# Attention into routed experts: first keys prepared in two column blocks, some of the opening work moved to GpSimd

## The chip, the cores and the metric

One core of a Trainium2 chip. The metric is the device time of one execution in microseconds (us). The engines are named as the profile names them: PE (TensorE matmuls) and PEld (its weight loads), DVE (VectorE), ACT (ScalarE), POOL (GpSimd), SP (SyncE, here a DMA queue). A q behind a name (SPq, ACTq, POOLq) is the engine's queue, from which it issues DMAs.

## What is computed

Attention over q, k, v of shape (8, 12, 448, 64), with queries and keys normalised over their 64 features, then a layer of eight experts that keeps at most 80 tokens per expert:

```python
def rmsnorm(x, g):
    return x / np.sqrt(np.mean(x * x, axis=-1, keepdims=True) + 1e-06) * g
scores = np.matmul(rmsnorm(q, g_q), rmsnorm(k, g_k).transpose(0, 1, 3, 2)) / np.sqrt(64)
attn = softmax(scores)                       # batch 8, heads 12, 448 x 448
x = matmul(attn, v)                          # to 3584 rows of 768
logits = x @ w_gate                          # 8 experts, the best one per row
# each expert keeps the 80 rows of the highest gate weight
out[rows] = gate * (np.maximum(x[rows] @ w1[e], 0) @ w2[e])
```

The product g_q * g_k / 8 is one vector over the 64 features. It can stand on either side of the score product, so the kernel applies it once, to one of the two.

## The kernel before

The attention goes in 24 groups (NG) of four heads. One tile of a group is 128 partitions by 14 blocks (NB) of 64 features: 64 row positions of two heads lie on the partitions, and the 14 blocks are two halves (head pairs `hh`) of seven columns x (NX). For each group:

- `load_qk` (line 259) loads q and k. The four buffers of the tag `qk` go round, so the load for group g+2 waits until group g's tile has been read. All these loads but two halves of group 0 are in SP's queue, in program order.
- `square` (278, ACT) and `squares` (285, DVE) make the sums of squares; `root` (293, ACT) and `inverse` (307, DVE) make 1/rms for group 0, `rstd` (298) does it for later groups by Ln and Exp on ACT and three small DVE operations; `normalise` (312, DVE) multiplies.
- `transp` (340) turns the normalised tile with 14 PE transposes into PSUM and copies it to `T0` (queries) or `T1` (keys) in SBUF. For group 0 the keys' copy, on DVE (line 355), applies the vector `gqk`.
- `score` (361) takes one column block x of keys: four matmuls into a PSUM tile `ps` (two buffers of the tag `sc`), then the exponential on ACT into `at`. `av` (375) multiplies `at` by v; `presum` (397, DVE) adds up the seven `at` tiles.

The order of the program is written out by hand. Slots s run from -10 to 89; slot s issues scores 2s and 2s+1, then the functions listed under `mid`, then the value products 2s-2 and 2s-1, then those under `end`. Lists `begins`, `mid`, `end`, `ahead` and `after` are filled by `at_slot`. Each engine works through its own instructions in program order.

Slot -10 (lines 721 to 728) prepares group 0 and, on ACT, squares the first tile of group 1 (`square(1, 0)`). Queries and keys of group 0 are squared, summed and normalised in halves `lo` and `hi`. `load_g` (81) has two small loads of g_q and g_k in ACT's queue; `gains` (88) multiplies them on POOL and turns the row into a PSUM column `gp` with a small matmul, `gained` (98) copies it to `gqk`. `exptable` (715) has ACT load its exponential table. PE begins with 12 matmuls on zeros (line 806, tile `wps`), and `stir` (101) issues more of them, three and two, between the transposes. Group 1 is squared, normalised and turned in slots -1 to 2, group 2 from slot 0 on.

While group 0 is being prepared, POOL sets constants (lines 126 to 175 and the identity for the transposes); `constants` (158) has DVE convert some of them.

Of the kernel before, what the change touches and what calls it, by code (L numbers as in the profile page):

```python
# [10 lines left out]
F32 = mybir.dt.float32  # L11
BF16 = mybir.dt.bfloat16
AF = mybir.ActivationFunctionType
# [8 lines left out]
def kernel(  # L22
# [13 lines left out]
    nc = tc.nc  # L36

    B, H, S, D = q.shape
# [9 lines left out]
    NX = S // 64  # L48
# [7 lines left out]
    NB = 2 * NX  # L56
# [7 lines left out]
    NW0 = 3  # L64
    wb_dram = nc.dram_tensor("wb_scratch", (E - NW0, 2, DM * F), BF16, kind="Internal").ap()

    cpool = ctx.enter_context(tc.tile_pool(name="const", bufs=1))

    warm = cpool.tile([1, 2], F32, name="warm")
# [9 lines left out]
    gk = []  # L79

    def load_g():
        gk.append(tpool.tile([128, 512], F32, tag="R", name="gk"))
        for t, src in enumerate((g_q, g_k)):
            nc.scalar.dma_start(
                out=gk[0][:1, t * 128:t * 128 + 128].rearrange("p (t d) -> p t d", t=2),
                in_=src[None, None, :].to_broadcast([1, 2, D]))

    def gains():

        t = gk[0]  # L90
        grow = t[:1, 256:384]
        nc.gpsimd.tensor_mul(grow, t[:1, 0:128], t[:1, 128:256])
        nc.gpsimd.tensor_scalar_mul(grow, grow, 1.0 / math.sqrt(D))
        gp = scps.tile([128, 2, 512], F32, tag="sc", name="gp")
        nc.tensor.matmul(gp[:, 0, 0:1], grow, one[:, :], start=True, stop=True)
        gk.extend((gp, wps))
# [30 lines left out]
    ZW = 192  # L127
    zeros = cpool.tile([128, ZW], F32, name="zeros")
    nc.vector.memset(zeros[:, :], 0.0)

    tpool = ctx.enter_context(tc.tile_pool(name="topk", bufs=1))

# [98 lines left out]
    tpps = ctx.enter_context(tc.tile_pool(name="tp_ps", bufs=1, space=PSUM))  # L231
# [3 lines left out]
    scps = ps_stack.enter_context(tc.tile_pool(name="sc_ps", bufs=2, space=PSUM))  # L235
# [9 lines left out]
    with av_stack:  # L245
# [3 lines left out]
        st = [dict() for _ in range(NG)]  # L249
# [28 lines left out]
        def square(g, a, parts=ALLB):  # L278
            if "sq%d" % a not in st[g]:
                st[g]["sq%d" % a] = qkpool.tile([128, NB, D], F32, tag="sq", name="sq", bufs=2)  # L280
            for lo, hi in parts:
                nc.scalar.activation(st[g]["sq%d" % a][:, lo:hi], st[g]["qk"][a][:, lo:hi],  # L282
                                     AF.Square)

        def squares(g, a, parts=ALLB):
            if "ms" not in st[g]:
                for n in ("ms", "rs", "nw"):
                    st[g][n] = prep.tile([128, 2, NB], F32, tag=n, name=n)
            for lo, hi in parts:
                nc.vector.reduce_sum(out=st[g]["ms"][:, a, lo:hi],  # L290
                                     in_=st[g]["sq%d" % a][:, lo:hi], axis=AX.X)

        def root(g, a, parts):
            for lo, hi in parts:
                nc.scalar.activation(st[g]["rs"][:, a, lo:hi], st[g]["ms"][:, a, lo:hi], AF.Sqrt,
                                     scale=1.0 / D, bias=eps[:, :])

        def rstd(g):
# [7 lines left out]

        def inverse(g, a, parts):
            for lo, hi in parts:
                rs = st[g]["rs"][:, a, lo:hi]
                nc.vector.reciprocal(rs, rs)  # L310

        def normalise(g, a, parts=ALLB):
            if "qn%d" % a not in st[g]:
                st[g]["qn%d" % a] = qkpool.tile([128, NB, D], F32, tag=f"qn{a}", name="qn", bufs=2)
            qn, qk, rs = st[g]["qn%d" % a], st[g]["qk"][a], st[g]["rs"][:, a]
            for lo, hi in parts:
                h0, h1 = lo // NX, hi // NX
                nc.vector.tensor_mul(  # L318
                    qn[:].rearrange("p (x hh) d -> p hh x d", hh=2)[:, h0:h1],
                    qk[:, lo:hi].rearrange("p (hh x) d -> p hh x d", x=NX),  # L320
                    rs[:, lo:hi].rearrange("p (hh x) -> p hh x", x=NX)
                    .unsqueeze(3).to_broadcast([128, h1 - h0, NX, D]))

        def turned(o, w, p):
            one = ident if w.dtype == F32 else identb
            nc.tensor.transpose(o, w, one[p, p], tile_position=(p.start, 0))  # L326
# [13 lines left out]
        def transp(g, a):  # L340

            if not a or g == 1:
                tp = tpps.tile([128, 2, 512], F32, tag="tp", name="tp")
            else:
                tp = scps.tile([128, 2, 512], F32, tag="sc", name="tp")
            qn = st[g]["qn%d" % a]
            T = qktpool.tile([128, 2, S], F32, tag=f"qkT{a}", name="qkT")
            st[g]["T%d" % a] = T
            for x in range(NX):
                for u in range(2):  # L350
                    p = slice(64 * u, 64 * u + 64)
                    turned(tp[:, u, x * 64:(x + 1) * 64],
                           qn[p, 2 * x:2 * x + 2, :].rearrange("p h d -> p (h d)"), p)
            if g == 0 and a:
                nc.vector.tensor_scalar_mul(T[:], tp[:, :, :S], gqk[:, :])
            elif a == (g == 0):
                nc.scalar.activation(T[:], tp[:, :, :S], AF.Copy, scale=gqk[:, :])  # L357
            else:
                nc.scalar.copy(T[:], tp[:, :, :S])  # L359

        def score(r):
            g, x = divmod(r, RD)
            T0, T1 = st[g]["T0"], st[g]["T1"]
# [343 lines left out]
        def at_slot(where, s, f, *a):  # L707
            where.setdefault(s, []).append((f, a))
# [11 lines left out]
        lo, hi = HALF  # L720
        for f, *a in ((square, 0, lo), (square, 0, hi), (squares, 0, lo), (root, 0, lo),
                      (square, 1, lo), (squares, 0, hi), (root, 0, hi), (square, 1, hi),
                      (lambda: square(1, 0), ), (inverse, 0, lo), (normalise, 0, lo), (inverse, 0, hi),
                      (normalise, 0, hi), (squares, 1, lo), (root, 1, lo), (squares, 1, hi),
                      (root, 1, hi), (transp, 0), (gains, ), (stir, 3, 2), (inverse, 1, lo),
                      (normalise, 1, lo), (inverse, 1, hi), (normalise, 1, hi), (gained, ),
                      (exptable, ), (transp, 1), (stir, 2, 1)):
            at_slot(mid, -10, f, *([0] if a and f is not stir else []), *a)
        for g in range(NG):
            b0 = g * RD // 2  # L730
            at_slot(begins, b0 - 11 if g > 1 else -10, load_qk, g)
            at_slot(begins, b0 - 4, load_v, g)
            if g:
                for a in range(2):
                    if a or g > 1:
                        at_slot(mid, b0 - 7 + a if g > 1 else -1, square, g, a)
                    at_slot(end, b0 - 7 + a if g > 1 else -1, squares, g, a)
                at_slot(mid, b0 - 5 if g > 1 else 0, rstd, g)
                for a in range(2):
                    s = b0 - 5 + a if g > 1 else 0  # L740
# [325 lines left out]
```

## Time and profile before

| | us |
|---|---|
| median of 3 runs | 418.39 |
| lowest and highest | 416.96, 419.76 |
| the profiled execution | 416.07 |
| span of its instructions | 414.4 |
| PE busy in the span | 399.3 |
| DVE busy | 355.9 |
| ACT busy | 315.4 |
| POOL busy | 82.0 |

The span runs from the first to the last instruction; 1.67 us of the profiled execution lie outside it. "Busy" counts instructions in work on an engine; a matmul's duration holds its passage through the array, so a string of matmuls overlaps. Rows give times from the start of the span.

### The profile page before, as it was taken

The page shows a single profiled execution, that of the slowest core. Times are in us where ns is not written, and L with a number is a line of the kernel's source. Part 1 is how long each engine was busy: PE and PEld are TensorE (multiplying, and loading weights), DVE is VectorE, ACT ScalarE, POOL GpSimd, SP SyncE. Part 2 cuts the span into 40 slices and gives each one's busy share as a digit, 9 for nine tenths or more (in the row PEclk, how much of TensorE's full clock was granted, in tenths as well). Part 3 has the DMA queues.
Part 4 walks back from the last instruction along what each step waited for, and adds up shares of the span by engine and source line. Part 5 has one row for each costly group of instructions (what it writes and reads, how often), then busy time and mean ns, then how long its engine had stood idle before and what let it go on. Part 6 is the DMA issues. An engine that isn't in the chain of part 4 may idle for free.

```text
span 414.4 us, 12611 instructions
## 1 busy us (share of the span) xinstructions
PE 399.3 (96%) x5299; PEld 196.8 (47%) x5299; DVE 355.9 (86%) x656; ACT 315.4 (76%) x482; POOL 82.0 (20%) x140
## 2 busy tenths in 40 slices
PE   8999999999999999999999999999999999889993
PEld 8434444444444445444443444444344444448882
DVE  7799887998999999989999999979999969735560
ACT  6898979997989699979899699978997784402111
POOL 3000002501040013121241025101502030134321
PEclk9999999999999999999999999999999999999997
DMA  7469998999989899989999999999899294989981
GB/s 261 143 163 227 260 322 170 277 218 294 245 235 276 226 256 270 295 187 251 245 314 225 235 265 267 255 228 303 206 228 292 54 338 165 258 256 341 346 297 47
DMA packets 75983, 100.91 MB, mean 244 GB/s; under 512 B 8344, under 2 KB 65176, under 8 KB 75928
## 3 DMA queue, kind: packets, MB, share of 16 engines
q1 hardware_dynamic: 59856, 70.53, 53.1%
q0 software_dynamic: 15776, 29.13, 38.8%
q8 instruction: 41, 0.67, 0.6%
q10 hardware_dynamic: 296, 0.46, 0.4%
q14 instruction: 14, 0.11, 0.1%
HBM read 101.11 MB, written 39.89 MB: 340 GB/s over the span
## 4 chain that ended last, share of the span: by engine, by line
PE 85%; DVE 4%; ACT 4%; DMA 3%; issue 2%; POOLq 0%; DVEq 0%
PE ps L369 30%; PE po L386 28%; PE zl L421 5%; PE py L1014 4%; PE tp L326 4%; PE ph L995 3%; PE xp L326 3%; DMA qk<-in_k_dram 2%; PE wps L806 2%; ACT at L372 1%; DMA xg<-xr_scratch,idxG 1%; PE mp L599 1%; ACT zsb L431 1%; ACT zo L433 1%; DVE sm L404 1%
## 5 line engine op out<-in xcount | busy, mean ns | idle before, releaser
L372 ACT ACTIVATE at<-ps 128x896 f32<-128x896 f32 x168 | 146.4, 930 | 4.8 <-PE ps L369 3.7
L369 PE MATMUL ps<-qkT 64*64 64x448 f32 x1344 | 147.2, 548 | 3.0 <-ACT row L553 1.3
L386 PE MATMUL po<-at,vt 64*64 64x448 f32 x1344 | 142.4, 537 | 0.0
L404 DVE TENSOR_TENSOR sm<-sm,at 128x896 f32<-128x896 f32 x120 | 130.5, 1087 | 3.1
L386 PEld LDWEIGHTS po<-at,vt 64*64 64x64 f32 x1344 | 50.0, 133 | 74.5 <-issue 64.5
L369 PEld LDWEIGHTS ps<-qkT 64*64 64x64 f32 x1344 | 43.4, 132 | 67.6 <-issue 25.8
L290 DVE TENSOR_REDUCE ms<-sq 128x14 f32<-128x896 f32 (+1 forms) x50 | 51.9, 1042 | 5.2 <-ACT sq L282 5.2
L318 DVE TENSOR_TENSOR qn<-qk,rs 128x896 f32<-128x896 f32 (+1 forms) x50 | 52.4, 1049 | 1.4
L282 ACT ACTIVATE sq<-qk 128x896 f32<-128x896 f32 (+1 forms) x50 | 46.3, 930 | 1.7 <-DMA qk<-in_q_dram 1.7
L999 ACT ACTIVATE h_sb<-ph 128x320 bf16<-128x320 f32 x16 | 7.0, 438 | 37.5 <-PE ph L995 37.5
L213 POOL COPY mark<-mark 1x1 bf16<-1x1 bf16 x20 | 7.5, 375 | 138.2 <-DVE mark L212 138.2
L666 ACT COPY xb<-xp 128x1024 f32<-128x1024 f32 x24 | 24.3, 1012 | 9.0 <-PE xp L326 8.6
L326 PEld LDWEIGHTS tp<-ident,qn 64*128 64x128 f32 x672 | 23.4, 139 | 11.4 <-ACT at L372 4.9
L326 PE MATMUL tp<-ident,qn 64*128 64x64 f32 x672 | 26.9, 226 | 0.1
L393 ACT COPY us<-po 128x896 f32<-128x896 f32 (+1 forms) x24 | 21.4, 894 | 6.9 <-PE po L386 6.9
L402 DVE TENSOR_TENSOR sm<-at 128x896 f32<-128x896 f32 x24 | 26.0, 1084 | 0.1
L357 ACT ACTIVATE qkT<-tp,gqk 128x896 f32<-128x896 f32 x23 | 23.6, 1025 | 0.0
L359 ACT COPY qkT<-tp 128x896 f32<-128x896 f32 x24 | 22.0, 917 | 1.5 <-PE tp L326 1.4
L1014 PE MATMUL py<-w_sb,h_sb 128*80 128x384 bf16 (+1 forms) x136 | 22.2, 317 | 0.0
L1018 DVE TENSOR_SCALAR yo<-py,gwT 80x384 f32<-80x384 f32 (+1 forms) x16 | 9.5, 601 | 13.9 <-PE py L1014 13.6
L421 PE MATMUL zl<-us,wgs 64*32 64x448 f32 x192 | 20.4, 540 | 0.0
L421 PE MATMUL zl<-sm,zsel 64*32 64x448 f32 x192 | 20.3, 540 | 0.0
(176 smaller groups left out, 425.1 us busy)
## 6 DMA issues: line engine op xcount, KB each, us to landing
wb_scratch<-in_moe_w_dram POOLq DMA_DIRECT2D x20, 768.0 KB, 10.3
w_sb<-wb_scratch SPq DMA_DIRECT2D x9, 1536.0 KB, 9.8
vt<-in_v_dram SPq DMA_DIRECT2D x24, 448.0 KB, 5.5
out_dram<-zeros SPq DMA_DIRECT2D x28, 384.0 KB, 9.0
qk<-in_q_dram SPq DMA_DIRECT2D x23, 448.0 KB, 5.7
qk<-in_k_dram SPq DMA_DIRECT2D x23, 448.0 KB, 5.9
w_sb<-in_moe_w_dram POOLq DMA_DIRECT2D x6, 1536.0 KB, 14.2
xr_scratch<-xb SPq DMA_DIRECT2D x48, 192.0 KB, 7.5
```

Source lines behind the costliest of these rows:

```text
L282: nc.scalar.activation(st[g]["sq%d" % a][:, lo:hi], st[g]["qk"][a][:, lo:hi], AF.Square)
L290: nc.vector.reduce_sum(out=st[g]["ms"][:, a, lo:hi], in_=st[g]["sq%d" % a][:, lo:hi], axis=AX.X)
L318: nc.vector.tensor_mul(qn[:].rearrange("p (x hh) d -> p hh x d", hh=2)[:, h0:h1], qk[:, lo:hi].rearrange("p (hh x) d -> p hh x d", x=NX), ...
L326: nc.tensor.transpose(o, w, one[p, p], tile_position=(p.start, 0))
L369: nc.tensor.matmul(ps[u * 64:u * 64 + 64, hh, :S], T1[d, u, x * 64:(x + 1) * 64], T0[d, u, :], start=True, stop=True)
L372: nc.scalar.activation(at[:], ps[:, :, :S], AF.Exp)
L386: nc.tensor.matmul(po[u][hh * D:(hh + 1) * D, u, :S], vt[p, hh * NX + x, :], at[p, hh, :], start=(x == 0), stop=(x == RD - 1))
L402: nc.vector.tensor_add(s["sm"][:], s["at0"][:], s["at1"][:])
L404: nc.vector.tensor_add(s["sm"][:], s["sm"][:], s["at%d" % x][:])
L421: nc.tensor.matmul(t[32 * c:32 * c + 32, r, :S], w, x, start=(i == 0), stop=(i == NQ - 1))
L666: nc.scalar.copy(xb[:].rearrange("p j (u hh d) -> p hh (j u) d", u=2, hh=2), xp[:].rearrange("p hh (k d) -> p hh k d", d=D))
L1014: nc.tensor.matmul(py[:, :c1 - c0], h_sb[:, fc, :], chunk(e, 1, fc)[:, c0:c1], start=(fc == 0), stop=(fc == FC - 1))
```

## The change

The two loads of g_q and g_k are issued by POOL, ahead of all its constants. The second half of group 0's queries is normalised on POOL; the product of the gains follows it on POOL, and its small matmul becomes a function of its own (`gproduct`). Group 1's squares are both made on POOL, in slot -10. Group 0's keys are summed in halves as before, get one reciprocal, and are then normalised, turned and copied in two blocks of columns: three columns (`keys_normal(0)`, `keys_turned(0)`) ahead of the first score, four with `keys_normal(1)` in slot -10 and `keys_turned(1)` in slot 0, behind scores 0 and 1. Score x of group 0 takes the block that holds its column. One zero matmul stands where three stood, and one where two stood. `rstd` and the normalising of group 1 go from slot 0 to slot 1; its queries' transposes go ahead of slot 2's value products; group 2's squares, `rstd` and normalising go one slot later.

```diff
+    tpool = ctx.enter_context(tc.tile_pool(name="topk", bufs=1))
+    def load_g():
+        gk.append(tpool.tile([128, 512], F32, tag="R", name="gk"))
+        for t, src in enumerate((g_q, g_k)):
+            nc.gpsimd.dma_start(
...
+    load_g()
     cpool = ctx.enter_context(tc.tile_pool(name="const", bufs=1))
...
-            nc.scalar.dma_start(
...
         nc.gpsimd.tensor_scalar_mul(grow, grow, 1.0 / math.sqrt(D))
+
+    def gproduct():
+        grow = gk[0][:1, 256:384]
         gp = scps.tile([128, 2, 512], F32, tag="sc", name="gp")
         nc.tensor.matmul(gp[:, 0, 0:1], grow, one[:, :], start=True, stop=True)
...
-    def stir(n, t):
-        for i in range(n):
-            nc.tensor.matmul(gk[t][:, 1, :ZW], zeros[:, :128], zeros[:, :], start=True, stop=True)
+    def stir(t):
+        nc.tensor.matmul(t[:, 1, :ZW], zeros[:, :128], zeros[:, :], start=True, stop=True)
...
-                nc.scalar.activation(st[g]["sq%d" % a][:, lo:hi], st[g]["qk"][a][:, lo:hi],
-                                     AF.Square)
+                o, x = st[g]["sq%d" % a][:, lo:hi], st[g]["qk"][a][:, lo:hi]
+                if g == 1:
+                    nc.gpsimd.tensor_mul(o, x, x)
+                else:
+                    nc.scalar.activation(o, x, AF.Square)
...
-                nc.vector.tensor_mul(
+                e = nc.gpsimd if g == 0 and h0 else nc.vector
+                e.tensor_mul(
...
+        KP = ((0, 3), (3, NX))
+        def keys_normal(n):
+            x0, x1 = KP[n]
...
+            nc.vector.tensor_mul(
+                qn[:].rearrange("p (x hh) d -> p hh x d", hh=2)[:, :, x0:x1],
+                st[0]["qk"][1][:].rearrange("p (hh x) d -> p hh x d", x=NX)[:, :, x0:x1],
+                st[0]["nw"][:, 1].rearrange("p (hh x) -> p hh x", x=NX)[:, :, x0:x1]
+                .unsqueeze(3).to_broadcast([128, 2, x1 - x0, D]))
+        def keys_turned(n):
...
+            for x in range(x0, x1):
+                for u in range(2):
+                    p = slice(64 * u, 64 * u + 64)
+                    turned(tp[:, u, x * 64:(x + 1) * 64],
+                           st[0]["qn1%d" % n][p, 2 * x:2 * x + 2, :].rearrange("p h d -> p (h d)"),
+                           p)
+            c = slice(64 * x0, 64 * x1)
+            nc.vector.tensor_scalar_mul(T[:, :, c], tp[:, :, c], gqk[:, :])
...
-                      (lambda: square(1, 0), ), (inverse, 0, lo), (normalise, 0, lo), (inverse, 0, hi),
-                      (normalise, 0, hi), (squares, 1, lo), (root, 1, lo), (squares, 1, hi),
-                      (root, 1, hi), (transp, 0), (gains, ), (stir, 3, 2), (inverse, 1, lo),
-                      (normalise, 1, lo), (inverse, 1, hi), (normalise, 1, hi), (gained, ),
-                      (exptable, ), (transp, 1), (stir, 2, 1)):
+                      (inverse, 0, lo), (normalise, 0, lo), (inverse, 0, hi),
+                      (normalise, 0, hi), (gains, ), (squares, 1, lo), (root, 1, lo), (squares, 1, hi),
+                      (root, 1, hi), (transp, 0), (lambda: stir(wps), ), (gproduct, ), (inverse, 1, ALLB),
+                      (keys_normal, 0), (gained, ), (keys_turned, 0), (exptable, ), (lambda: stir(gk[1]), ),
+                      (keys_normal, 1), (lambda: square(1, 0), ), (lambda: square(1, 1), ),
+                      (lambda: squares(1, 0), )):
...
+        at_slot(mid, 0, keys_turned, 1)
+        at_slot(mid, 0, squares, 1, 1)
...
-                at_slot(mid, b0 - 5 if g > 1 else 0, rstd, g)
+                late = g == 2
+                for a in range(2 if g > 1 else 0):
+                    at_slot(mid, b0 - 7 + a + late, square, g, a)
+                    at_slot(end, b0 - 7 + a + late, squares, g, a)
+                at_slot(mid, b0 - 5 + late if g > 1 else 1, rstd, g)
...
-                    at_slot(end, b0 - 2 + (a if g == 1 else 0), transp, g, a)
+                    if g == 1:
+                        at_slot(end if a else mid, b0 - 1, transp, g, a)
+                    else:
+                        at_slot(end, b0 - 2, transp, g, a)
...
-        at_slot(begins, -10, load_g)
```

## Rows read from the trace of the kernel before

**Rows 1.** The page: busy time by engine, granted clock by slice, the chain that ended last.

```profile
PE 399.3 (96%) x5299; PEld 196.8 (47%) x5299; DVE 355.9 (86%) x656; ACT 315.4 (76%) x482; POOL 82.0 (20%) x140
...
PEclk9999999999999999999999999999999999999997
...
PE 85%; DVE 4%; ACT 4%; DMA 3%; issue 2%; POOLq 0%; DVEq 0%
```

**Rows 2.** Timeline of PE: start, length, engine, line, out<-in, count [idle before <-releaser].

```profile
1.59 6.84 PE L806 MATMUL wps<-zeros 128*128 128x192 f32 x24 [1.59 <-DVE zeros L129]
8.36 0.65 PE L326 MATMUL tp<-ident,qn 64*128 64x64 f32 x14
9.00 0.38 PE L95 MATMUL gp<-one,gk 1*128 1x1 f32 x2
...
10.61 0.65 PE L326 MATMUL tp<-ident,qn 64*128 64x64 f32 x14
...
12.60 1.73 PE L369 MATMUL ps<-qkT 64*64 64x448 f32 x16 [0.49 <-DVE qkT L355]
14.61 1.79 PE L369 MATMUL ps<-qkT 64*64 64x448 f32 x16 [0.28 <-ACT at L372]
...
21.58 0.65 PE L326 MATMUL tp<-ident,qn 64*128 64x64 f32 x14
...
31.66 1.08 PE L326 MATMUL tp<-ident,qn 64*128 64x64 f32 x28
```

**Rows 3.** Timeline of DVE, the opening and group 2's keys.

```profile
2.62 0.89 DVE L163 CAST numF<-numI 128x8 f32<-128x8 int32 x1
5.06 1.15 DVE L290 TENSOR_REDUCE ms<-sq 128x7 f32<-128x448 f32 x2 [1.56 <-ACT sq L282]
...
6.35 0.62 DVE L318 TENSOR_TENSOR qn<-qk,rs 128x448 f32<-128x448 f32 x1
...
7.66 1.14 DVE L290 TENSOR_REDUCE ms<-sq 128x7 f32<-128x448 f32 x2
...
9.72 0.63 DVE L318 TENSOR_TENSOR qn<-qk,rs 128x448 f32<-128x448 f32 x1
...
11.30 1.15 DVE L355 TENSOR_SCALAR qkT<-tp,gqk 128x896 f32<-128x896 f32 x1 [0.89 <-PE tp L326]
...
27.45 1.08 DVE L318 TENSOR_TENSOR qn<-qk,rs 128x896 f32<-128x896 f32 x1
```

**Rows 4.** Timeline of ACT around its table load.

```profile
9.06 0.91 ACT L359 COPY qkT<-tp 128x896 f32<-128x896 f32 x1
9.98 1.28 ACT L716 ACT_TABLE_LOAD   x1
...
13.64 1.73 ACT L372 ACTIVATE at<-ps 128x896 f32<-128x896 f32 x2 [1.32 <-PE ps L369]
```

**Rows 5.** Timeline of POOL in the opening.

```profile
3.19 0.29 POOL L170 TENSOR_SCALAR_AFFINE_SELECT tri<-tri 128x128 bf16<-128x128 bf16 x1
7.84 0.45 POOL L92 TENSOR_TENSOR gk<-gk 1x128 f32<-1x128 f32 x1 [4.37 <-DMA gk<-in_g_k_dram]
8.38 0.56 POOL L93 TENSOR_SCALAR gk<-gk 1x128 f32<-1x128 f32 x1
```

**Rows 6.** Groups of instructions on POOL: count | busy us, mean ns | idle before.

```profile
L216 POOL DMA_DIRECT2D wb_scratch<-in_moe_w_dram x20 | 15.3, 763 | 0.7
...
L522 POOL TENSOR_TENSOR info<-eq,pt 128x160 bf16<-128x160 f32 x8 | 3.9, 482 | 0.6
```

**Rows 7.** Timeline of DVE and POOL at 334 to 338 us.

```profile
334.21 2.19 DVE L404 TENSOR_TENSOR sm<-sm,at 128x896 f32<-128x896 f32 x2
...
335.41 1.05 POOL L529 TENSOR_TENSOR left<-gw,pt 128x4 f32<-128x4 f32 x1
...
336.80 0.21 POOL L531 TENSOR_TENSOR pt<-left,pt 128x4 bf16<-128x4 f32 x1
```

**Rows 8.** Stretches: length, busy (count) of PE, PEld, DVE, ACT, POOL, granted clock, DMA share, GB/s.

```profile
12.00:13.00 1.00, 0.51 (x6) 0.24 (x9) 1.00 (x2) 0.32 (x1) 0.00 (x0) 1.00 1.03 384
...
60.00:100.00 40.00, 39.89 (x542) 17.20 (x540) 36.11 (x61) 35.95 (x52) 7.53 (x10) 1.00 0.99 244
```

More of the change, by code (lines that the diff above doesn't have):

```diff
@@ L77 @@
     nc.vector.memset(one[:, :], 1.0)
[L79 to L83, printed above, removed]
-            nc.scalar.dma_start(
-                out=gk[0][:1, t * 128:t * 128 + 128].rearrange("p (t d) -> p t d", t=2),
-                in_=src[None, None, :].to_broadcast([1, 2, D]))
     def gains():
@@ L294, in root @@
             for lo, hi in parts:
-                nc.scalar.activation(st[g]["rs"][:, a, lo:hi], st[g]["ms"][:, a, lo:hi], AF.Sqrt,
+                nc.scalar.activation(st[g][("rs", "nw")[a]][:, a, lo:hi],
+                                     st[g]["ms"][:, a, lo:hi], AF.Sqrt,
                                      scale=1.0 / D, bias=eps[:, :])
@@ L308, in inverse @@
             for lo, hi in parts:
-                rs = st[g]["rs"][:, a, lo:hi]
+                rs = st[g][("rs", "nw")[a]][:, a, lo:hi]
                 nc.vector.reciprocal(rs, rs)
@@ L322, in normalise @@
                     .unsqueeze(3).to_broadcast([128, h1 - h0, NX, D]))
+        KP = ((0, 3), (3, NX))
+        def keys_normal(n):
+            x0, x1 = KP[n]
+            qn = qkpool.tile([128, NB, D], F32, tag="qn1", name="qn", bufs=2)
+            st[0]["qn1%d" % n] = qn
+            nc.vector.tensor_mul(
[4 more added lines that the diff above has]
+        def keys_turned(n):
+            x0, x1 = KP[n]
+            if n:
+                tp = tpps.tile([128, 2, 512], F32, tag="tp", name="tp")
+            else:
+                tp = scps.tile([128, 2, 512], F32, tag="sc", name="tp")
+            T = qktpool.tile([128, 2, S], F32, tag="qkT1", name="qkT")
+            st[0]["T1%d" % n] = T
+            for x in range(x0, x1):
[6 more added lines that the diff above has]
+            nc.vector.tensor_scalar_mul(T[:, :, c], tp[:, :, c], gqk[:, :])
         def turned(o, w, p):
@@ L353, in transp @@
                            qn[p, 2 * x:2 * x + 2, :].rearrange("p h d -> p (h d)"), p)
-            if g == 0 and a:
-                nc.vector.tensor_scalar_mul(T[:], tp[:, :, :S], gqk[:, :])
-            elif a == (g == 0):
+            if g and not a:
                 nc.scalar.activation(T[:], tp[:, :, :S], AF.Copy, scale=gqk[:, :])
@@ L362, in score @@
             g, x = divmod(r, RD)
-            T0, T1 = st[g]["T0"], st[g]["T1"]
+            T0 = st[g]["T0"]
+            T1 = st[g]["T1" if g else "T1%d" % (x >= KP[1][0])]
             ps = scps.tile([128, 2, 512], F32, tag="sc", name="ps")
@@ L722 @@
                       (square, 1, lo), (squares, 0, hi), (root, 0, hi), (square, 1, hi),
-                      (lambda: square(1, 0), ), (inverse, 0, lo), (normalise, 0, lo), (inverse, 0, hi),
-                      (normalise, 0, hi), (squares, 1, lo), (root, 1, lo), (squares, 1, hi),
-                      (root, 1, hi), (transp, 0), (gains, ), (stir, 3, 2), (inverse, 1, lo),
-                      (normalise, 1, lo), (inverse, 1, hi), (normalise, 1, hi), (gained, ),
-                      (exptable, ), (transp, 1), (stir, 2, 1)):
-            at_slot(mid, -10, f, *([0] if a and f is not stir else []), *a)
+                      (inverse, 0, lo), (normalise, 0, lo), (inverse, 0, hi),
[4 more added lines that the diff above has]
+                      (lambda: squares(1, 0), )):
+            own = f in (keys_normal, keys_turned)
+            at_slot(mid, -10, f, *([0] if a and not own else []), *a)
+        at_slot(mid, 0, keys_turned, 1)
+        at_slot(mid, 0, squares, 1, 1)
         for g in range(NG):
@@ L733 @@
             if g:
-                for a in range(2):
-                    if a or g > 1:
-                        at_slot(mid, b0 - 7 + a if g > 1 else -1, square, g, a)
-                    at_slot(end, b0 - 7 + a if g > 1 else -1, squares, g, a)
-                at_slot(mid, b0 - 5 if g > 1 else 0, rstd, g)
-                for a in range(2):
-                    s = b0 - 5 + a if g > 1 else 0
+                late = g == 2
[3 more added lines that the diff above has]
+                at_slot(mid, b0 - 5 + late if g > 1 else 1, rstd, g)
+                for a in range(2):
+                    s = b0 - 5 + a + late if g > 1 else 1
                     at_slot(after if not a and g % NQ == 0 and g > NQ else mid, s, normalise, g, a)
```

7 lines of the change are left out of this document (5 added, 2 removed).

## The prediction

> **What bounds the kernel now.** I read the page first, then the timelines of the opening engine by engine, then the stretches. On the page PE is busy for 96% of the span and carries 85% of the chain that ended last [rows 1]. From 60 to 100 us it is busy for 39.89 of 40 us while the DMA engines are busy throughout, so there it waits for no transfer [rows 8]. An edit that touches the first slots alone can therefore move the end only by bringing PE's unbroken run forward, and what it brings forward there should arrive at the end almost unchanged. The place to read is where that run starts.
>
> Before 12.60 PE does warm-up, transposes and zero matmuls; the first scores start at 12.60, 0.49 after PE's last work, released by the keys' copy on DVE [rows 2]. That copy (11.30, 1.15 long) follows the transposes of 10.61, and these follow DVE's multiply of 9.72 to 10.35 [rows 2, 3]. DVE is then the bound of the opening: from 5.06 to 10.35 it works through sums, reciprocals and four multiplies almost without a gap, starting when ACT hands over the first squares [rows 3]. The second pair of scores starts at 14.61, released by the exponentials, which began at 13.64 [rows 2, 4]. So the stage to re-time is DVE's from 5 to 12 us, then whatever DVE and POOL owe to PE up to 31.66, where group 2's transposes stand [rows 2].
>
> **The opening on DVE and POOL.** The second query multiply (0.62, some 0.55 in a pipelined string) leaves DVE, so the two key sums (1.14) start at 7.1 instead of 7.66 and end at 8.25 [rows 3]. From the first sum's end (half of 1.15 after 5.06, that is 5.65) to its multiply at 6.35 lie 0.7 us for root, reciprocal and hand-overs [rows 3]; so the first keys' multiply could start at 8.95. It has 384 elements where the half had 448: 0.56 by proportion. The one reciprocal of 14 in place of two of 7 changes nothing beyond that.
>
> POOL's price is not in the trace for this size. A two-input operation of four elements took 0.21 when nothing stood against it and one of 160 took 0.48 [rows 6, 7]; the line through both is 0.2 plus 1.75 ns an element, so 1.0 for 448 and 1.75 for 896. Below, I bound it by the single-row operation of 128 elements at 0.45 as a fixed price (0.45 and 0.45) [rows 5]; above, by proportion to the 160 (1.35 and 2.7) [rows 6]. I take 1.0 and 1.85, nearest to the line. The Trainium skill (GPSIMD Engine Reference, Performance versus the Vector engine) holds such work to be VectorE's and gives 4497 ns for 2048 elements; by it, as an estimate, 896 cost 1.97, 0.1 more than I take.
>
> The query half then runs on POOL from 7.15 to 8.15. PE cannot turn the queries before 8.36 anyway, because its warm-up lasts until then [rows 2], so this multiply is hidden; without that cover it would delay only the queries, whose copy ends at 9.97 and is not needed before the first score [rows 4]. The gains follow on POOL, 1.10 for the pair (7.84 to 8.94 before) [rows 5]: 8.15 to 9.25. The gain loads, which held them until 7.84, are no longer on the path.
>
> **The shared resource.** In the stretch at 334 us a four-element operation of POOL issued at 335.41 lasted 1.05, until DVE's pair of two-input additions had ended at 336.40; right after, its like took 0.21 [rows 7]. The other way round, a DVE cast of eight elements took 0.89 and ended at 3.51, when POOL's last constant ended at 3.48 [rows 3, 5]. I read this as: one of the two waits while the other has an operation in hand. The Trainium skill (Advanced Engine Details and Errata, GPSIMD Details) says that Pool shares a read and a write interface with DVE and conflicts with its operations of two SBUF inputs. The rows agree for POOL waiting; that a multiply of DVE waits for a long operation of POOL is in no row, and it is the choice on which my size hangs.
>
> I take it that it does. Then the first keys' multiply waits for the gains: 9.25 to 9.85. Six transposes by proportion to 14 in 0.65, with the last one's passage, 0.4: to 10.3 [rows 2]. The copy of 384 from PSUM, scaled from 1.15 for 896, 0.6: to 10.9 [rows 3]. First score at 10.95 against 12.60 [rows 2]: 1.65 earlier. The exponential table is loaded by 11.26 [rows 4] and the first score needs about 1.04 to its exponential (12.60 to 13.64), so 12.0: the load stays hidden, with some 0.7 left for the small exponential behind it.
>
> **Between the first scores and group 1.** Behind scores 0 and 1 (to 12.7) PE has eight transposes of the second key block, 0.4, then score 2 at 13.1. POOL squares group 1's queries from 9.85 to 11.7; `keys_normal(1)` (512 elements, 0.7) waits for it: to 12.4. Then `squares(1, 0)` stands ahead of the second block's copy in DVE's queue: 1.05, to 13.45, and the copy (0.7) ends at 14.15. Score 3 waits for it, about 0.15 behind PE. Value products start at 15.0; before, PE reached them at 14.61 + 1.6 = 16.2 [rows 2]. So 1.2 are left: added waits that were absent before, on POOL and in DVE's queue, take 0.45 of the 1.65.
>
> POOL's second square runs 12.4 to 14.25, its sum to 15.3, one addition to 16.35, the small operations of `rstd` to 17.2, the multiply of group 1's queries to 18.25. PE finishes scores 4 and 5 at 18.0, so their transposes wait 0.25. They now stand ahead of the value products; the keys' transposes come at 20.4 against 21.58 [rows 2]: 1.15 earlier.
>
> For group 2, DVE has from 19.3 on ten operations of about 1.05 and 0.7 of small ones until the keys of group 2 are ready: 30.5. Before, they were ready at 28.53 [rows 3] and turned at 31.66 [rows 2]; with PE 1.15 earlier they are wanted at 30.5. The cover of 3.1 us is used up by the move of one slot, and any further lateness of DVE shows there. On SP's queue the load of the third group's queries waits for POOL's half (8.15), its keys' load for `keys_normal(1)`: 12.4, two later than the last multiply of 10.35 [rows 3]; both are first needed after 16 us. The loads behind them follow; nothing reads them before slot 3.
>
> **Edits at nothing.** Issuing the gain loads on POOL: 0.76 for one of 768 KB [rows 6], bounded below by the 0.21 of the smallest POOL operation and above by twice 0.76; two push POOL's constants, and with them DVE's casts, which ended at 3.51, by 0.4 to 3.0, of which 1.55 are free before 5.06 [rows 3]. I take 1.5: no cost. The squares and the DMA issues that ACT loses were not on the path. The three zero matmuls fewer leave PE idle in pieces below a microsecond; the clock is granted in full also in the stretch where PE was busy for 0.51 of 1 us [rows 8]. Later stages do not change.
>
> **Sum.** 1.65 - 0.45 - 0.1 = 1.1 us off the profiled execution's 416.07, so 415.0 (span 413.3). The median of the runs shown is 418.39, 2.3 above that execution, and the forecast is for a median: 417.3. About 1% (4.2 us) is what a measurement of this kernel can tell from no change; this is a quarter of it.
>
> **Rivals.** *DVE does not wait for POOL.* Then the first keys' multiply ends at 9.5, the gains' column lands at 9.65, scores start at 10.7, group 1's transposes wait little, and group 2 is ready 0.6 sooner: 1.7 off, 416.7. For it: DVE's two-input additions kept their usual length beside POOL at 334 us [rows 7]; against it: the cast of 0.89 [rows 3]. Chance 0.22.
>
> *POOL's squares become the bound (the other side).* Two squares in series stand before group 1's `rstd`. Each 0.1 us more apiece costs about 0.2 at group 1's transposes; the gain of 1.1 is gone at 2.4 us each, and at 2.7, the proportional bound [rows 6], the kernel is 0.6 slower: 419.0. For it: POOL's four-element operation of 1.05 beside DVE [rows 7]; against it: the line through the unhindered ones. Chance 0.18.
>
> *POOL's opening DMAs are dear.* At 1.1 each (0.76 is the mean with 768 KB [rows 6]) the casts end at 5.7, the sums start 0.65 late, and 0.45 is left: 417.9. Chance 0.12. *The clock falls* when PE idles between small pieces: 32 score matmuls of 1.73 and 1.79 [rows 2] at half speed, of which the exponentials' pace hides some 1.5: 2 lost, 0.9 slower, 419.3. The full grant at half occupancy speaks against it [rows 8]. Chance 0.05.
>
> *The gain is given back later*, because DVE (86% busy [rows 1]) falls behind at group 2 or at a buffer: no change, 418.4. Chance 0.08. My own case keeps 0.35.
>
> **How the numbers follow.** All cases lie between 416.7 and 419.3; the three runs of before spread over 2.8, so a median is uncertain by about 1 either way. Range 415.0 to 419.4; my own case alone 416.2 to 418.4. Below 414.2 needs more than all the opening's idle time gives (0.07); above 422.6 needs POOL at several times its bound or a long spell at low clock (0.04); within 1%: 0.89.
>
> **What would show it.** First score near 10.95, DVE's keys' multiply lengthened or delayed to POOL's end, a POOL square near 1.85, group 1's key transposes near 20.4, group 2's near 30.5, and PE unbroken after. Wrong if POOL's 896 exceed 2.4, if DVE's first sum starts past 5.3, if the granted clock drops below full before 20 us, or if the lead at 31 us is lost by 100 us.

## The result and the profile after

The changed kernel took 423.32 us (median of 6 runs, 421.95 to 424.82) against 417.42 for the kernel before (median of 6; the 418.39 above is that of its first 3): ratio 1.0132, 95% interval 1.0098 to 1.0166. It is slower by 1.3%, where the forecast was 1.1 us faster. The profiled execution took 421.95, its span is 420.2 against 414.4.

PE's timeline shows where. The columns are those of [rows 2].

```profile
8.29 0.65 PE L363 MATMUL tp<-ident,qn 64*128 64x64 f32 x14 [0.37 <-POOL qn L326]
...
13.15 0.58 PE L363 MATMUL tp<-ident,qn 64*128 64x64 f32 x6 [3.38 <-DVE gqk L104]
...
14.78 3.27 PE L405 MATMUL ps<-qkT 64*64 64x448 f32 x16
...
18.59 2.24 PE L405 MATMUL ps<-qkT 64*64 64x448 f32 x16
...
26.43 0.65 PE L363 MATMUL tp<-ident,qn 64*128 64x64 f32 x14
...
36.51 1.08 PE L363 MATMUL tp<-ident,qn 64*128 64x64 f32 x28
```

PE stood still for 3.38 us ahead of the first keys' transposes. The first scores start at 14.78 (12.60 before), and the pair takes 3.27 instead of 1.73. Group 1's keys are turned at 26.43 instead of 21.58, group 2's at 36.51 instead of 31.66: 4.85 late. From there little more is lost for 290 us (0.24, then 0.05 regained): the first gate matmuls of the eight batches come 5.09 late (61.76 against 56.67), the last 5.04 (353.34 against 348.30). The remaining 0.8 of the span's 5.8 lie behind that, 0.5 of them in the first gather of rows (4.01 against 3.49), which takes between 3.49 and 4.33 over the profiles of all these kernels.

The bracket names the copy of the gains' column, and that copy only stood in DVE's queue behind something else. DVE's timeline, to be read against [rows 3]:

```profile
5.18 1.15 DVE L296 TENSOR_REDUCE ms<-sq 128x7 f32<-128x448 f32 x2
...
7.12 1.09 DVE L296 TENSOR_REDUCE ms<-sq 128x7 f32<-128x448 f32 x2
...
8.86 4.15 DVE L338 TENSOR_TENSOR qn<-qk,nw 128x384 f32<-128x384 f32 x1
12.93 0.14 DVE L104 COPY gqk<-gp 128x1 f32<-128x1 f32 x1
13.77 0.62 DVE L359 TENSOR_SCALAR qkT<-tp,gqk 128x384 f32<-128x384 f32 x1 [0.70 <-PE tp L363]
14.31 0.68 DVE L338 TENSOR_TENSOR qn<-qk,nw 128x512 f32<-128x512 f32 x1
```

The first keys' multiply was ready at 8.86, as forecast (8.95), and lasted 4.15. Its sister of 512 elements, larger, lasted 0.68. The difference stands in POOL's timeline:

```profile
7.29 0.94 POOL L326 TENSOR_TENSOR qn<-qk,rs 128x448 f32<-128x448 f32 x1 [1.97 <-DVE rs L317]
...
8.74 0.56 POOL L95 TENSOR_SCALAR gk<-gk 1x128 f32<-1x128 f32 x1
9.28 3.31 POOL L287 TENSOR_TENSOR sq<-qk 128x896 f32<-128x896 f32 x2
```

POOL's two squares run from 9.28 to 12.59, and the multiply ends at 13.01, 0.42 later. By the profile the multiply had started first, 0.42 before the squares, and that did not help it. The clock then shows in the stretches (columns of [rows 8]):

```profile
12.00:13.00 1.00, 0.00 (x0) 0.00 (x0) 1.00 (x2) 0.00 (x0) 0.59 (x1) 0.92 0.00 0
13.00:14.00 1.00, 0.85 (x7) 0.76 (x8) 0.30 (x3) 0.00 (x0) 0.00 (x0) 0.50 0.00 0
...
18.00:19.00 1.00, 1.00 (x15) 0.78 (x16) 0.29 (x1) 0.90 (x1) 0.00 (x0) 0.50 0.81 301
...
20.00:21.00 1.00, 1.00 (x16) 0.34 (x12) 1.00 (x2) 0.85 (x2) 0.00 (x0) 1.00 0.08 16
```

The granted clock fell while PE still stood (0.92 over the stretch from 12 to 13) and is 0.50, that is 1.2 GHz of 2.4, until past 19 us. So the theory after the result has two links: DVE's multiply of two SBUF inputs waits for POOL's run of operations as a whole, not for the one in hand; and PE's standstill then costs it half its clock for the first scores.

### The profile page after: what moved, and what is told of

The parts are those of the page before. It is cut to its first block, busy times and chain, and to the rows that moved or that the text cites. A ratio compares the mean times of both kernels' runs of the same rounds, so it can differ in the third digit from the quotient of the medians.

```text
span 420.2 us, 12599 instructions
## 1 busy us (share of the span) xinstructions
PE 401.0 (95%) x5293; PEld 196.1 (47%) x5293; DVE 358.7 (85%) x655; ACT 314.0 (75%) x480; POOL 87.2 (21%) x145
## 4 chain that ended last, share of the span: by engine, by line
PE 86%; ACT 5%; DVE 4%; issue 2%; DMA 1%; POOL 1%; POOLq 0%
PE ps L405 32%; PE po L422 29%; PE zl L457 5%; PE py L1056 4%; PE tp L363 4%; PE xp L363 3%; PE ph L1037 3%; ACT at L408 2%; DVE qn L338 1%; DMA xg<-xr_scratch,idxG 1%; PE mp L635 1%; ACT zsb L467 1%; ACT zo L469 1%; ACT xb L702 1%; PE mp L363 1%
## 5 line engine op out<-in xcount | busy, mean ns | idle before, releaser
L405 PE MATMUL ps<-qkT 64*64 64x448 f32 x1344 | 149.3, 554 | 2.3 <-ACT row L589 1.3
L326 DVE TENSOR_TENSOR qn<-qk,rs 128x896 f32<-128x896 f32 (+1 forms) x47 | 50.5, 1076 | 1.3
L289 ACT ACTIVATE sq<-qk 128x896 f32<-128x896 f32 (+1 forms) x48 | 44.5, 930 | 1.9 <-DMA qk<-in_q_dram 1.9
```

Source lines behind the costliest of these rows:

```text
L289: nc.scalar.activation(o, x, AF.Square)
L326: e.tensor_mul(qn[:].rearrange("p (x hh) d -> p hh x d", hh=2)[:, h0:h1], qk[:, lo:hi].rearrange("p (hh x) d -> p hh x d", x=NX), rs[:, lo ...
L405: nc.tensor.matmul(ps[u * 64:u * 64 + 64, hh, :S], T1[d, u, x * 64:(x + 1) * 64], T0[d, u, :], start=True, stop=True)
```

## The experiments

**The squares back on ACT.** All else stays as changed; the first square stands where it stood before the change, the second in slot 0.

```diff
-                if g == 1:
-                    nc.gpsimd.tensor_mul(o, x, x)
-                else:
-                    nc.scalar.activation(o, x, AF.Square)
+                nc.scalar.activation(o, x, AF.Square)
...
+                      (lambda: square(1, 0), ),
...
-                      (keys_normal, 1), (lambda: square(1, 0), ), (lambda: square(1, 1), ),
+                      (keys_normal, 1),
...
+        at_slot(mid, 0, square, 1, 1)
```

> Theory (port): the first keys' multiply on DVE waits until POOL's whole string of operations has ended (the gains and both squares of group 1, to 12.59). With the squares back on ACT it waits for the gains alone: length about 1.0 instead of 4.15, end near 9.9, first score near 11.0, granted clock 1.00 throughout, the kernel 1.2 us faster than before (ratio 0.997). Rival (shape): the multiply of three columns in two strided halves is slow in itself; it keeps its 4.15 and the kernel stays 5 to 6 us slower than before. Rival (too few zero matmuls): the multiply is short, but the clock falls to half all the same near 13 us, and the kernel is about 1 us slower than before.

Timelines of DVE, POOL and PE:

```profile
9.03 0.56 DVE L335 TENSOR_TENSOR qn<-qk,nw 128x384 f32<-128x384 f32 x1
...
8.76 0.56 POOL L95 TENSOR_SCALAR gk<-gk 1x128 f32<-1x128 f32 x1
...
10.94 1.74 PE L402 MATMUL ps<-qkT 64*64 64x448 f32 x16 [0.28 <-DVE qkT L356]
...
30.79 1.09 PE L360 MATMUL tp<-ident,qn 64*128 64x64 f32 x28
```

The multiply takes 0.56, the first score starts at 10.94, the granted clock is 1.00 in every stretch from 8 to 22 us, group 2's transposes come 0.87 before those of [rows 2]. The ratio is 0.9962, interval 0.9935 to 0.9990 (416.35 against 417.86), near the 0.997 expected. Both rivals fall: neither the shape nor the smaller number of zero matmuls is the cause. One detail also went against me: the multiply did not wait even for the gains, which POOL had in hand until 9.32.

**More zero matmuls.** The changed kernel with PE's standstill filled:

```diff
-                      (root, 1, hi), (transp, 0), (lambda: stir(wps), ), (gproduct, ), (inverse, 1, ALLB),
+                      (root, 1, hi), (transp, 0), (lambda: stir(wps), ), (gproduct, ),
+                      *[(lambda: stir(wps), )] * 10, (inverse, 1, ALLB),
```

> The changed kernel with ten more zero matmuls in PE's idle time, nothing else. Theory: the multiply still lasts 4.15, but the granted clock stays 1.00 from 13 to 20 us, the first two scores take 1.75 instead of 3.27, group 2's transposes come near 34.5 instead of 36.5, and about 2 of the 5.9 us come back (ratio to before 1.009). Rival (the exponentials pace the scores anyway): the clock stays full and less than 0.5 us comes back.

PE's timeline:

```profile
9.69 3.52 PE L107 MATMUL wps<-zeros 128*128 128x192 f32 x20
...
14.47 1.74 PE L405 MATMUL ps<-qkT 64*64 64x448 f32 x16 [0.28 <-DVE qkT L359]
...
34.13 1.08 PE L363 MATMUL tp<-ident,qn 64*128 64x64 f32 x28
```

The multiply lasts 4.15 as before, the clock stays at 1.00, the first pair of scores takes 1.74, and group 2's transposes come at 34.13: 2.38 of the 4.85 us belong to the clock. The ratio to before is 1.0034 (1.0015 to 1.0053) where 1.009 was expected; the rival of less than 0.5 falls. In whole runs the return is larger than in the profiles (1.0132 to 1.0034): the profiled execution of the changed kernel was its fastest, at a mean granted clock of 0.986, and its three slowest have 0.983. Whether that is the whole of the difference is not shown.

So the 4.85 at group 2's transposes are 3.34 lost by having the squares on POOL ahead of the multiply (34.13 less 30.79; the multiply alone is 3.59 longer, 4.15 against 0.56), plus 2.38 lost by the clock, less 0.87 that the other parts give.

**How DVE gets in: four runs.** The first lets POOL's second square wait for a mark that DVE sets behind the first keys' multiply.

```diff
+    def opened():
+        nc.vector.memset(mark[:, 0:1], 0.0)
+    def passed():
+        nc.gpsimd.tensor_copy(mark[:, 0:1], mark[:, 0:1])
...
-                      (keys_normal, 0), (gained, ), (keys_turned, 0), (exptable, ), (lambda: stir(gk[1]), ),
-                      (keys_normal, 1), (lambda: square(1, 0), ), (lambda: square(1, 1), ),
+                      (keys_normal, 0), (opened, ), (gained, ), (keys_turned, 0), (exptable, ),
+                      (lambda: stir(gk[1]), ),
+                      (keys_normal, 1), (lambda: square(1, 0), ), (passed, ), (lambda: square(1, 1), ),
```

> POOL's second square waits for a mark that DVE sets behind the first keys' multiply. Theory (port, string): DVE comes in at the gap after the first square: multiply lasts 2.6 to 2.7 (end near 11.5) instead of 4.15, second square starts near 11.6. Rival (shape): 4.15 as before, the second square then starts near 13. Whether the clock falls after a PE idle time of some 1.8 us instead of 3.4 is open; if it stays full, the first score is near 12.3 and group 2's transposes near 33.

Timelines of DVE and POOL:

```profile
8.79 2.50 DVE L344 TENSOR_TENSOR qn<-qk,nw 128x384 f32<-128x384 f32 x1
...
12.41 1.33 DVE L344 TENSOR_TENSOR qn<-qk,nw 128x512 f32<-128x512 f32 x1
...
9.20 1.67 POOL L293 TENSOR_TENSOR sq<-qk 128x896 f32<-128x896 f32 x1
11.38 0.18 POOL L107 COPY mark<-mark 1x1 bf16<-1x1 bf16 x1 [0.51 <-DVE gqk L110]
11.53 1.67 POOL L293 TENSOR_TENSOR sq<-qk 128x896 f32<-128x896 f32 x1
```

The first square ends at 10.87, the multiply at 11.29: again 0.42 behind. The second keys' multiply then met the second square: it lasted 1.33, where 0.68 is usual, and ended at 13.74, 0.54 behind that square. PE's standstill was 1.74 here, and the clock fell none the less, later and for a shorter time. PE's timeline and a stretch:

```profile
11.44 0.40 PE L369 MATMUL tp<-ident,qn 64*128 64x64 f32 x6 [1.74 <-DVE gqk L110]
...
13.00:14.00 1.00, 1.00 (x12) 0.51 (x8) 1.00 (x2) 0.15 (x1) 0.20 (x1) 0.66 0.00 0
14.00:15.00 1.00, 1.00 (x8) 0.00 (x0) 0.74 (x1) 0.77 (x1) 0.00 (x0) 0.50 0.16 25
```

The second run makes the second square twice.

```diff
-                      (keys_normal, 1), (lambda: square(1, 0), ), (lambda: square(1, 1), ),
+                      (keys_normal, 1), (lambda: square(1, 0), ), (lambda: square(1, 1), ),
+                      (lambda: square(1, 1), ),
```

> The changed kernel with the second of POOL's squares made twice. Theory (port, string): the multiply grows by one square, 1.66, to 5.8; first score near 16.4; group 2's transposes near 38.2. Rival (DVE waits for one operation only, or is slow by its shape): 4.15 as it was, first score near 14.8.

Timelines of DVE and POOL:

```profile
8.72 4.15 DVE L338 TENSOR_TENSOR qn<-qk,nw 128x384 f32<-128x384 f32 x1
...
9.14 5.26 POOL L287 TENSOR_TENSOR sq<-qk 128x896 f32<-128x896 f32 x3
```

The third square alone, from a stretch that leaves the others out:

```profile
12.52 1.88 POOL L287 TENSOR_TENSOR sq<-qk 128x896 f32<-128x896 f32 x1
```

They contradict the expectation: 4.15, the rival's number, not 5.8. The three squares take 5.26, that is 1.95 more than two, where a square takes 1.67: the third starts some 0.07 after the second has ended and lasts 0.21 longer than the others. The program's order offers a reason: the third writes the tile that the second wrote and carries a wait for POOL's own second operation; the second carries none for the first. Either DVE came in where POOL stopped for that wait, or it is let in after a certain number of operations. The third run tells these apart: it cuts the squares in halves, four operations without a wait among them.

```diff
-                      (keys_normal, 1), (lambda: square(1, 0), ), (lambda: square(1, 1), ),
+                      (keys_normal, 1),
+                      *[(lambda a=a, p=p: square(1, a, p), ) for a in range(2) for p in HALF],
```

> The changed kernel with each of POOL's two squares cut in two halves: four operations of some 0.93 in a row, none of which waits for another of POOL. Theory (string): DVE comes in only where POOL stops to wait, so the first keys' multiply lasts until about 0.4 after the fourth, 4.4 to 4.6 long. Rival (count: DVE is let in after two further operations, as the run with a third square could be read): 2.6 to 2.8 long, the last halves lengthened.

Timelines of DVE and POOL:

```profile
8.96 4.43 DVE L338 TENSOR_TENSOR qn<-qk,nw 128x384 f32<-128x384 f32 x1
...
9.38 3.59 POOL L287 TENSOR_TENSOR sq<-qk 128x448 f32<-128x448 f32 x4
```

The multiply outlasts all four halves (12.97) by 0.42. The count falls. The fourth run puts one small copy between the two whole squares that reads the first one's result, so that POOL waits for itself and for nothing of DVE.

```diff
+        def drained():
+            nc.gpsimd.tensor_copy(mark[:, 0:1], st[1]["sq0"][:1, NB - 1, D - 1:D])
...
-                      (keys_normal, 1), (lambda: square(1, 0), ), (lambda: square(1, 1), ),
+                      (keys_normal, 1), (lambda: square(1, 0), ), (drained, ), (lambda: square(1, 1), ),
```

> The changed kernel with one small copy on POOL between its two squares, which reads the last element of the first square's result and so waits for that square, and for nothing of DVE. Theory (DVE comes in where POOL stops to wait, for whatever reason): the first keys' multiply lasts 2.5, as with the mark of DVE, and ends near 11.3. Rival (only a POOL wait on DVE itself lets DVE in): 4.2 to 4.4.

Timelines of DVE and POOL:

```profile
8.74 2.51 DVE L341 TENSOR_TENSOR qn<-qk,nw 128x384 f32<-128x384 f32 x1
...
9.16 1.67 POOL L287 TENSOR_TENSOR sq<-qk 128x896 f32<-128x896 f32 x1
10.89 0.40 POOL L333 CAST mark<-sq 1x1 bf16<-1x1 f32 x1
11.25 1.67 POOL L287 TENSOR_TENSOR sq<-qk 128x896 f32<-128x896 f32 x1
```

2.51: a stop of POOL on its own result is enough. The copy that follows lasts 0.40, where a copy of one element took 0.18 in the first of these runs, and ends 0.04 after the multiply, which fits POOL waiting for DVE there. With these four, each one profiled execution, the mechanism is settled in its outward form: DVE's multiply waits until POOL stops, however many operations that takes.

Why POOL comes first is open. POOL's queue was done with the waits ahead of its two squares just before the multiply started at 8.86; the changed kernel's trace, by line, has for the squares

```profile
L287 POOLq EVENT_SEMAPHORE  x2: 17/17/17, 8.7 to 8.8; - x2
```

In the run with halves these waits were done at 8.8 to 8.9 and the multiply started at 8.96. So the engine whose operation was issued first may be the one that goes first. At 334 us, where DVE's additions were under way first, POOL's operation was the one that waited [rows 7]. No run makes DVE's multiply the earlier one beside the squares, so this is not shown.

**Squares on POOL, but behind the keys.** Both squares wait for a mark set behind `keys_normal(1)`, and the first one's sum goes behind the second key block's copy.

```diff
-                      (keys_normal, 1), (lambda: square(1, 0), ), (lambda: square(1, 1), ),
-                      (lambda: squares(1, 0), )):
+                      (keys_normal, 1), (opened, ), (passed, ), (lambda: square(1, 0), ),
+                      (lambda: square(1, 1), )):
...
+        at_slot(mid, 0, squares, 1, 0)
```

> The changed kernel with both squares still on POOL, but held by a mark that DVE sets behind the second keys' multiply, and the sum of the first of them put behind the second key block's copy. Theory: the first keys' multiply takes 0.56, the first score starts near 10.95, the clock stays full; group 1's sums end near 16, its queries' transposes come near 18.9 and its keys' near 21; 0.7 to 1.2 us faster than before (ratio 0.997 to 0.998). Rival (POOL's squares are too slow in any place): group 1's transposes come after 20 and the kernel is not faster than before.

The multiply takes 0.59, the first score starts at 11.19, group 1 is turned at 19.03 and 21.28. PE's timeline has group 2 0.3 ahead of [rows 2]:

```profile
19.03 0.65 PE L369 MATMUL tp<-ident,qn 64*128 64x64 f32 x14 [0.78 <-DVE qn L332]
...
31.36 1.09 PE L369 MATMUL tp<-ident,qn 64*128 64x64 f32 x28
```

The ratio is 1.0004 (0.9980 to 1.0028): the loss is gone, a gain is not shown. Both sides are missed in part. Group 1 is turned before 20, so POOL is fast enough not to lose there. The gain that was expected is not shown: group 2 is 0.57 later than with the squares on ACT (31.36 against 30.79).

**The other parts, one at a time,** all on the kernel with the squares on ACT. Group 2's work back in its former slots:

```diff
-                late = g == 2
+                late = 0
```

> The kernel with the squares back on ACT, and group 2's work put back in the slots it had before. Theory (DVE's order binds there): the sum of group 2's first square comes ahead of group 1's normalising on DVE, so group 1's queries are turned about 1.0 later (19.5 instead of 18.46), and most of that is still there at group 2's transposes (31.5 instead of 30.8). Rival (the later slots are a loss or nothing): group 1's transposes keep 18.5 and group 2's come no later than 30.8.

PE's timeline:

```profile
19.45 0.65 PE L360 MATMUL tp<-ident,qn 64*128 64x64 f32 x14 [1.35 <-DVE qn L323]
...
31.77 1.08 PE L360 MATMUL tp<-ident,qn 64*128 64x64 f32 x28
```

Against 18.46 and 30.79 the later slots are worth 1.0 in the traces, as expected. The second half of the queries back on DVE:

```diff
-                e = nc.gpsimd if g == 0 and h0 else nc.vector
+                e = nc.vector
```

> The kernel with the squares on ACT, and the second half of the queries normalised on DVE again. Theory of the prediction (0.55 of DVE's string saved): the key sums start 0.55 later (7.7), the first keys' multiply at 9.5, the first score at 11.4 to 11.5 instead of 10.94. Rival (the half on POOL saves nothing): first score within 0.15 of 10.94.

DVE's timeline has the key sums at 7.86, and the first score starts at 11.54: POOL's half is worth 0.60 (11.54 less 10.94).

```profile
7.86 1.13 DVE L293 TENSOR_REDUCE ms<-sq 128x7 f32<-128x448 f32 x2
```

The gains' loads back on ACT went wrong at first, since with this edit alone they stood ahead of ACT's loads of queries and keys:

```diff
-            nc.gpsimd.dma_start(
+            nc.scalar.dma_start(
```

> The kernel with the squares on ACT, and the two loads of the gains back in ACT's queue. Theory (the loads on POOL cost nothing): DVE's first sum starts within 0.15 of 5.2, the first keys' multiply and the first score (10.94) stay within 0.15, the time as with the loads on POOL. Rival (POOL's loads push the opening): the constants end 1.8 earlier, the first sum at 5.05 or before, the first score 0.2 or more earlier.

ACT's timeline shows the second half of the queries being squared only once it had landed, at 8.42 instead of about 5.1; the first score started at 15.62. This run says nothing on POOL's loads, only what two loads of 0.5 KB cost at the head of a queue (1.22 and 0.57 to issue).

```profile
0.80 1.22 ACTq L73 DMA_DIRECT2D gk<-in_g_q_dram  x1
2.05 0.57 ACTq L73 DMA_DIRECT2D gk<-in_g_k_dram  x1
...
8.42 0.58 ACT L286 ACTIVATE sq<-qk 128x448 f32<-128x448 f32 x1 [3.81 <-DMA qk<-in_q_dram]
```

With the call also back behind those loads:

```diff
-            nc.gpsimd.dma_start(
+            nc.scalar.dma_start(
...
-    load_g()
...
+        at_slot(begins, -10, load_g)
```

> The kernel with the squares on ACT, and the two loads of the gains in ACT's queue behind the loads of queries and keys, where they stood before the change. Theory (the loads on POOL cost nothing): POOL's constants end at 3.5 instead of 5.3, DVE's casts with them, yet the first sum still starts at 5.05 to 5.2 because it waits for ACT's first square; the gains have landed before POOL wants them (8.2); first score within 0.2 of 10.94; ratio to before 0.995 to 0.998. Rival (the loads on POOL push the opening, or on ACT push the squares): first score 0.3 or more away from 10.94, either way.

DVE's timeline:

```profile
4.90 1.15 DVE L292 TENSOR_REDUCE ms<-sq 128x7 f32<-128x448 f32 x2 [1.39 <-ACT sq L285]
```

The first sum starts at 4.90 and waits for ACT's square; the first score starts at 10.77, 0.17 earlier than with the loads on POOL. So these loads cost next to nothing. The ratio is 1.0001 (0.9975 to 1.0027), with group 2 turned at 30.61; the expected ratio of 0.995 to 0.998 was not met.

**An attempt at the best of both.** Gains and their matmul ahead of POOL's half of the queries, the first square on ACT, the second on POOL behind a mark.

```diff
-                if g == 1:
+                if g == 1 and a:
...
-        for f, *a in ((square, 0, lo), (square, 0, hi), (squares, 0, lo), (root, 0, lo),
+        for f, *a in ((gains, ), (square, 0, lo), (square, 0, hi), (squares, 0, lo), (root, 0, lo),
...
+                      (lambda: square(1, 0), ),
...
-                      (normalise, 0, hi), (gains, ), (squares, 1, lo), (root, 1, lo), (squares, 1, hi),
-                      (root, 1, hi), (transp, 0), (lambda: stir(wps), ), (gproduct, ), (inverse, 1, ALLB),
+                      (normalise, 0, hi), (squares, 1, lo), (root, 1, lo), (squares, 1, hi),
+                      (root, 1, hi), (gproduct, ), (transp, 0), (lambda: stir(wps), ), (inverse, 1, ALLB),
...
-                      (keys_normal, 1), (lambda: square(1, 0), ), (lambda: square(1, 1), ),
+                      (keys_normal, 1), (opened, ), (passed, ), (lambda: square(1, 1), ),
```

> The gains and their small matmul ahead of POOL's half of the queries, group 1's first square on ACT as before the change, its second on POOL behind a mark that DVE sets after the second keys' multiply. Theory: first keys' multiply 0.56, first score near 10.8, the sum of the second square near 13.9 instead of 14.6, no wait at group 1's transposes, group 2's near 30.2 instead of 30.8; 1.8 to 2.2 us faster than before (ratio 0.995). Rival (POOL's square holds up DVE there too): group 1's transposes after 18.5 and no gain over the kernel with both squares on ACT.

The timelines of POOL and DVE tell why it missed:

```profile
7.01 0.45 POOL L94 TENSOR_TENSOR gk<-gk 1x128 f32<-1x128 f32 x1 [1.70 <-DMA gk<-in_g_k_dram]
...
8.10 0.93 POOL L332 TENSOR_TENSOR qn<-qk,rs 128x448 f32<-128x448 f32 x1
...
8.65 0.80 DVE L344 TENSOR_TENSOR qn<-qk,nw 128x384 f32<-128x384 f32 x1
```

The gains had not landed before 7.0, although POOL issued their loads from 1.34 on, and now POOL's half of the queries queued behind them: first score at 11.52, ratio 1.0017 (0.9990 to 1.0044). That half, one operation on two different tensors, also held up the first keys' multiply: 0.80 where 0.56 was expected, ending at 9.45, once more 0.42 behind POOL (9.03). So it is not only squares, with the same tensor as both inputs, that do it. The transposes of group 1 at 18.86 and the missing gain are what the rival said, but not for its reason: the loss came before POOL's square ran (12.21).

The squares on ACT thus remain the one part to undo. Whether that version beats the kernel before is near the limit of what can be measured: its interval lies below 1, that of the nearly equal version with the loads on ACT does not, and both profiled executions have a span of 413.9 against 414.4. The traces give 0.9 to 1.05 us at group 2's transposes.

## Why the prediction was wrong

**What held.** PE's run is unbroken from group 1's transposes on, and what the opening loses arrives at the end (4.85 at 36 us, 5.04 at 353). DVE is the bound of the opening; its string loses 0.55 with the query half (0.60 measured at the first score); the key sums end and the multiply is ready where I had them (8.86 for 8.95); POOL's half takes 0.94 (1.0), a square 1.67 (1.85); the loads on POOL cost next to nothing. With the squares off POOL the first score starts at 10.94, where I had 10.95, though by two errors that cancel: I let the multiply wait for the gains, which it did not, and had too little for the steps between it and the score (1.10, measured 1.35). The multiply's 0.56 was met too, though the proportion to 0.62 that I named gives 0.53.

**The step that failed** is in the shared resource: "one of the two waits while the other has an operation in hand", and from it "the first keys' multiply waits for the gains: 9.25 to 9.85. [...] POOL squares group 1's queries from 9.85". I had the direction right, gave it as the choice on which the size hangs, and then let DVE in at the next boundary between two POOL operations. The runs show that there is no such boundary unless POOL stops: 4.15 behind two squares, 4.43 behind four halves, 2.50 and 2.51 where POOL stopped after one. Having the squares in that place cost 3.34 at group 2's transposes, where I had 0.3 for the wait before the first score and 0.45 behind it.

The rows had a hint. The cast of 0.89, from 2.62 to 3.51, that I read as waiting for one operation outlasted POOL's last four constants one after another, of which [rows 5] shows the last. It has one input, and whether it waited at all no run shows. And the rows at 334 us [rows 7] show POOL's operations one at a time only because each there waits for the one before. I took a chain with waits in it for the rule.

The Trainium skill (GPSIMD Engine Reference, Instruction dispatch) says that each of GpSimd's cores starts its share of the next operation as soon as it has finished its share of the last. By that, back-to-back operations without a wait leave no gap; the traces agree, with 3.31 for two squares that take 1.67 alone. That a waiting DVE operation is kept out for the whole run of them is shown by the runs alone.

**The clock** was a rival with a chance of 0.05 and a price of 2, set against the row with PE half busy [rows 8]. Its price was right (2.38), its chance was not: I treated it as an accident beside the waits, while here it followed from one. The multiply's extra 3.59 on DVE became a standstill of 3.38 on PE. The 423.32 lie above the 422.6 for which I wanted POOL at several times its bound or a long spell at low clock (chance 0.04); it was a wait in the wrong place and a spell of some 7 us. With the clock at full grant the kernel would still have been 0.3% slower.

**The other rivals.** POOL's squares did become the bound, but not by the price I gave that case: they were faster than I took them to be (1.67 against the 2.4 from which I had it decide). What decided is their place in POOL's queue, right behind the gains and ahead of DVE's multiply. Group 2, for which I saw the cover used up, was not late: its later slots are worth 1.0.

## What to carry to other kernels

Before work goes to GpSimd, list which VectorE operations with two SBUF inputs become ready while GpSimd has a run of operations that do not wait for one another: in this kernel such an operation was held up for the whole rest of the run, behind two-input POOL operations of 448 and 896 elements. Place the run behind the operations that the path needs, by a dependence and not by program order alone, or keep the work on an engine without this conflict. And price a new wait of the matmul engine twice: its length, and half-speed matmuls after it, until the full clock is granted again.

## What the runs showed of the hardware that was not expected

- A DVE multiply of two SBUF inputs (128x384, 0.56 by itself) lasted 2.50 to 4.43 beside POOL's squares and 0.80 beside POOL's multiply of 448, always to 0.42 or 0.43 after POOL's unbroken run had ended. DVE's sums of one input beside POOL's 0.94 multiply took 1.09 for two, no more than the 1.15 with POOL idle [rows 3].
- It was not held up by POOL's one-row multiplication by a constant: 0.56 when it started at 9.03 while that one ran (8.76 to 9.32).
- After a standstill of PE of 1.74 to 1.75 us the granted clock fell to 0.50 some 2 us later, while PE was at work on the first scores again. In the changed kernel it fell during the standstill of 3.38; with that one filled by zero matmuls it stayed at 1.00. The shorter standstill was filled in no run.
- Two loads of 0.5 KB issued by POOL at 1.34 and 2.06 as the first DMAs of its queue had landed for POOL's use only at 7.0, with the loads of queries and keys under way at the same time.
